# One row map instead of three, no short first loads, and loads held for gamma, in a layer-scale kernel

## The chip, the cores and the metric

The kernel runs on one core of a Trainium2 chip. The metric is device time in microseconds (us); three runs of the kernel before gave 119.6, 119.63 and 119.88 us, so its median is 119.63 us.

## The reference

`x` and `y` have the shape 1024 x 16 x 512 in bf16, `gamma` has 512 elements. All that is computed is one multiply and one add per element:

```python
def reference(x, y, gamma):
    return x + gamma * y
```

Flattened, `x`, `y` and the output are 16384 rows of 512 elements, 1 KB a row and 16.78 MB a tensor. Two tensors are read and one is written: 50.33 MB.

## The kernel before, in words

**Row map.** Each of the 128 SBUF partitions owns 128 rows, 128 KB of each tensor. Which rows is set by `BLOCKS = [4, 64, 60]` (line 7): the tensor is cut into three consecutive blocks of 128x4, 128x64 and 128x60 rows, and in a block partition p owns the p-th run of 4, 64 or 60 consecutive rows (`rows_of`, line 65). Two neighbouring partitions therefore read 4 KB, 64 KB or 60 KB apart in HBM, and a load of a whole block is one unbroken region of HBM.

**Buffers.** `y_sb` holds all 128 rows of a partition. A product is written over `y` and a sum over the product, so `y_sb` is also what is stored. `x_sb` holds 76 rows; the last number of an `x` load says where it goes. The loads of rows 68 to 120 and 120 to 128 overwrite rows of earlier loads and wait for the adds that read them (`frees`, line 102, and the wait on `s_add`, line 126).

**Queues.** `SP` (line 12) lists the loads that SyncE issues, `ACT` (line 20) the DMAs that ScalarE issues: the first four rows of `x`, `gamma` as one row of 1 KB, and three stores. The order is written out by hand, and `ring` (line 113) walks each list. All three stores wait for `s_go`, which TensorE gives once the load named in `RELEASE`, `x` rows 68 to 120, has landed (lines 157 and 158).

**Start.** `EARLY = (2, 1)` moves the first two SP loads and the first ACT load to the very beginning of the program, ahead of the barriers. `HOLD, AHEAD = ('y', 0, 4), (2, 1)` hold everything behind them, `gamma` included, until the four-row load of `y` has landed: TensorE waits for that load (line 147) and then raises one semaphore for each of SP, ACT and VectorE.

**Gamma.** A matmul of a column of ones with the row `gamma_row` spreads it over 128 partitions in PSUM (line 152), and VectorE copies it to `gamma_sb` (line 154).

**Compute.** VectorE does all elementwise work in pieces of 8, 16, 44, 52 and 8 rows (`PIECES`, line 9), in the order written in `DVE` (line 28): the multiplies (line 180) of pieces 0, 1, 2, the adds (line 189) of pieces 2, 0, 1, the multiplies of 3 and 4, the adds of 3 and 4.

Of the kernel before, what the change touches and what calls it, by code (L numbers as in the profile page):

```python
# [3 lines left out]

BLOCKS = [4, 64, 60]

PIECES = [8, 16, 44, 52, 8]


SP = [
    ('y', 0, 4),
    ('y', 4, 68),
    ('x', 4, 68, 4),
    ('y', 68, 128),
    ('x', 68, 120, 24),
    ('x', 120, 128, 0),
]
ACT = [('x', 0, 4, 0), ('g',), ('s', 4, 68), ('s', 0, 4), ('s', 68, 128)]  # L20

EARLY = (2, 1)

HOLD, AHEAD = ('y', 0, 4), (2, 1)

RELEASE = ('x', 68, 120, 24)

DVE = [('m', 0), ('m', 1), ('m', 2), ('a', 2), ('a', 0), ('a', 1), ('m', 3), ('m', 4), ('a', 3), ('a', 4)]
MULT, ADD = mybir.AluOpType.mult, mybir.AluOpType.add
# [2 lines left out]
def _take(sem, n, eng):  # L32


    return eng.wait_ge(sem, n).then_inc(sem, -n)  # L35


def kernel(
# [9 lines left out]
    nc = tc.nc  # L48
# [8 lines left out]
    rows = N // P  # L57
    n = len(PIECES)
    assert sum(PIECES) == rows
    starts = [sum(PIECES[:c]) for c in range(n + 1)]  # L60
    dt = xf.dtype
    edges = [sum(BLOCKS[:c]) for c in range(len(BLOCKS) + 1)]
    assert edges[-1] == rows

    def rows_of(t, a, b):

        c = max(c for c in range(len(BLOCKS)) if edges[c] <= a)
        assert b <= edges[c + 1]
# [6 lines left out]
    y_sb = nc.alloc_sbuf_tensor("y_sb", [P, rows, D], dt).ap()  # L75
    x_loads = [w for w in ACT + SP if w[0] == "x"]
    y_loads = [w for w in SP + ACT if w[0] == "y"]
    stores = [w for w in SP + ACT if w[0] == "s"]
    for loads in (x_loads, y_loads, stores):
# [7 lines left out]
    s_load = {w: sem("s_" + "_".join(map(str, w[:2]))) for w in x_loads + y_loads}  # L87
    s_held = {nc.sync: sem("s_held_sp"), nc.scalar: sem("s_held_act"), nc.vector: sem("s_held_dve")}
# [4 lines left out]
    def meets(a, b, c, d):  # L93
        return a < d and c < b
# [4 lines left out]
    def x_at(row):  # L99
        return next(w[3] + row - w[1] for w in x_loads if w[1] <= row < w[2])  # L100
# [12 lines left out]
    def ring(eng, what, n_early, n_ahead):  # L113

        known, went = 0, False
        for k, w in enumerate(what):
            kind = w[0]
            if k == n_ahead:
                _take(s_held[eng], 1, eng)
            need = frees(w) if kind == "x" else pieces_of(w[1], w[2]) + list(w[3:]) if kind == "s" else []  # L120
            need = max((order[c] + 1 for c in need), default=0)
            if kind == "s" and not went:
                _take(s_go, 1, eng)
                went = True
            if need > known:
                eng.wait_ge(s_add, need)
                known = need
            if kind == "g":
                i = eng.dma_start(out=gamma_row, in_=gamma.unsqueeze(0)).then_inc(s_gamma, 16)
            elif kind == "x":  # L130
                to = x_sb[:, w[3] : w[3] + w[2] - w[1], :]
                i = eng.dma_start(out=to, in_=rows_of(xf, w[1], w[2])).then_inc(s_load[w], 16)
            elif kind == "y":
                r = slice(w[1], w[2])
                i = eng.dma_start(out=y_sb[:, r, :], in_=rows_of(yf, w[1], w[2])).then_inc(s_load[w], 16)
            else:
                r = slice(w[1], w[2])
                i = eng.dma_start(out=rows_of(of, w[1], w[2]), in_=y_sb[:, r, :]).then_inc(s_out, 16)
            if k < n_early:
                early.append(i.ins)  # L140

    ring(nc.sync, SP, EARLY[0], AHEAD[0])
    ring(nc.scalar, ACT, EARLY[1], AHEAD[1])


    nc.vector.memset(ones_row, 1.0).then_inc(s_ones, 1)  # L146
    _take(s_load[HOLD], 16, nc.tensor)
    for s_one in s_held.values():
        nc.tensor.sem_inc(s_one, 1)
    _take(s_ones, 1, nc.tensor)  # L150
    _take(s_gamma, 16, nc.tensor)
    nc.tensor.matmul(gamma_ps, ones_row, gamma_row, start=True, stop=True).then_inc(s_ps, 1)  # L152
    _take(s_ps, 1, nc.vector)
    nc.vector.tensor_copy(out=gamma_sb, in_=gamma_ps).then_inc(s_dve, 1)  # L154
    _take(s_dve, 1, nc.vector)

    _take(s_load[RELEASE], 16, nc.tensor)
    nc.tensor.sem_inc(s_go, 1)
# [4 lines left out]
    def need(loads, c):  # L163
        for w in loads:
            if w not in landed and meets(starts[c], starts[c + 1], w[1], w[2]):
                if w == RELEASE:
                    _take(s_rel, 1, nc.vector)
                elif w == HOLD:
                    _take(s_held[nc.vector], 1, nc.vector)
                else:  # L170
                    _take(s_load[w], 16, nc.vector)
                landed.add(w)

    for kind, *args in DVE:
        c = args[0]
        yt = y_sb[:, starts[c] : starts[c + 1], :]
        if kind == "m":
            need(y_loads, c)
            g = gamma_sb[:, None, :].to_broadcast([P, PIECES[c], D])
            nc.vector.tensor_tensor(out=yt, in0=yt, in1=g, op=MULT).then_inc(s_dve, 1)  # L180
            open_mults += 1
        else:
# [4 lines left out]
            at = x_at(starts[c])  # L187
            xt = x_sb[:, at : at + PIECES[c], :]
            nc.vector.tensor_tensor(out=yt, in0=xt, in1=yt, op=ADD).then_inc(s_add, 1)  # L189
# [44 lines left out]
```

## Time and profile before

| what | value |
|---|---|
| median of three runs | 119.63 us (119.6 to 119.88) |
| span of the profiled execution | 118.2 us |
| runs' median less that span (around the span) | 1.4 us |
| VectorE busy | 70.1 us, 59% of the span |
| TensorE busy | 0.6 us |
| DMA | 50.33 MB, 426 GB/s over the span |
| first multiply starts | 23.95 us |
| first add starts | 43.45 us |
| first store issued | 77.41 us |
| matmul of gamma starts | 11.59 us |

The span runs from the first to the last instruction of the program. The page gives no separate whole time for the profiled execution, so 1.4 us is the distance from its span to the median of the runs. In the views below, DVE is VectorE, SPq and ACTq are the instruction streams of SyncE and ScalarE that issue DMAs, and q1 and q10 are the DMA queues that they feed. Sixteen DMA engines serve both queues. A DMA is cut into packets; the trace has start, duration, queue and size of each, and a load over 128 partitions is 128 packets, one for each partition, eight on each engine.

### The profile page before, as it was taken

The numbers are of one execution on the slowest core, as the hardware profiler recorded it, in microseconds if no ns is written. First come the engines' busy times: TensorE is split into PE (matmuls) and PEld (weight loads), VectorE is DVE, ScalarE is ACT, GpSimd is POOL, SyncE is SP. The second block draws the span as 40 slices with busy tenths as digits, with TensorE's granted clock in tenths as the row PEclk, the third lists the DMA queues.
The fourth block names the chain that finished last, engine by engine and source line by source line (L and its number), as shares of the span: only waits on it lengthen the run. The fifth ranks groups of instructions, "written<-read, shape, count | busy, mean of one in ns | idle before, by whom it ended". The sixth has DMA issues, their size and how long they took to land. (4 is left out here: it accounts for less than half of the span.)

```text
span 118.2 us, 91 instructions
## 1 busy us (share of the span) xinstructions
PE 0.6 (0%) x1; PEld 0.1 (0%) x1; DVE 70.1 (59%) x12; POOL 0.2 (0%) x4
## 2 busy tenths in 40 slices
PE   0000100000000000000000000000000000000000
PEld 0000000000000000000000000000000000000000
DVE  0000200089999969999999999999999900000000
POOL 0000000000000000000000000000000000000000
DMA  6999889988899879879969696898899889799793
GB/s 248 461 666 399 355 355 399 665 355 355 355 599 466 355 333 624 374 333 499 499 288 576 288 576 288 360 637 355 355 576 488 355 355 510 333 582 416 333 499 166
DMA packets 1442, 50.33 MB, mean 426 GB/s; under 512 B 161, under 2 KB 162, under 8 KB 546
## 3 DMA queue, kind: packets, MB, share of 16 engines
q1 hardware_dynamic: 864, 33.03, 64.8%
q10 hardware_dynamic: 578, 17.30, 33.9%
HBM read 33.56 MB, written 16.78 MB: 426 GB/s over the span
## 5 line engine op out<-in xcount | busy, mean ns | idle before, releaser
L180 DVE TENSOR_TENSOR y_sb<-y_sb,gamma_sb 128x4096 bf16<-128x4096 bf16 (+3 forms) x5 | 34.7, 6981 | 10.9 <-DVEq L35 10.9
L189 DVE TENSOR_TENSOR y_sb<-x_sb,y_sb 128x4096 bf16<-128x4096 bf16 (+3 forms) x5 | 34.7, 6981 | 1.2 <-DVEq L35 1.1
L154 DVE CAST gamma_sb<-gamma_ps 128x512 bf16<-128x512 f32 x1 | 0.7, 692 | 10.2 <-DVEq L35 10.2
L146 DVE MEMSET ones_row<- 1x128 bf16 x1 | 0.2, 165 | 2.0 <-PEq L51 2.0
L152 PE MATMUL gamma_ps<-gamma_row,ones_row 1*128 1x512 bf16 x1 | 0.6, 581 | 11.6 <-PEq L35 11.6
L152 PEld LDWEIGHTS gamma_ps<-gamma_row,ones_row 1*128 1x128 bf16 x1 | 0.1, 101 | 11.6 <-issue 11.6
L218 POOL MEMSET const-bfloat16-1.0<- 128x1 bf16 x1 | 0.1, 101 | 0.0
L218 POOL MEMSET const-uint8-127<- 128x1 uint8 x1 | 0.1, 101 | 0.0
L218 POOL MEMSET const-float32-0.0<- 128x1 f32 x1 | 0.1, 98 | 0.2 <-issue 0.2
L218 POOL MEMSET const-float32-1.0<- 128x1 f32 x1 | 0.1, 98 | 0.0
## 6 DMA issues: line engine op xcount, KB each, us to landing
y_sb<-in_y_dram SPq DMA_DIRECT2D x1, 7680.0 KB, 57.3
out_dram<-y_sb ACTq DMA_DIRECT2D x1, 7680.0 KB, 23.8
x_sb<-in_x_dram SPq DMA_DIRECT2D x1, 6656.0 KB, 21.7
x_sb<-in_x_dram SPq DMA_DIRECT2D x1, 1024.0 KB, 22.0
y_sb<-in_y_dram SPq DMA_DIRECT2D x1, 512.0 KB, 3.4
x_sb<-in_x_dram ACTq DMA_DIRECT2D x1, 512.0 KB, 4.2
out_dram<-y_sb ACTq DMA_DIRECT2D x1, 512.0 KB, 22.3
y_sb<-in_y_dram SPq DMA_DIRECT2D x1, 23.4
```

Source lines behind the costliest of these rows:

```text
L146: nc.vector.memset(ones_row, 1.0).then_inc(s_ones, 1)
L152: nc.tensor.matmul(gamma_ps, ones_row, gamma_row, start=True, stop=True).then_inc(s_ps, 1)
L154: nc.vector.tensor_copy(out=gamma_sb, in_=gamma_ps).then_inc(s_dve, 1)
L180: nc.vector.tensor_tensor(out=yt, in0=yt, in1=g, op=MULT).then_inc(s_dve, 1)
L189: nc.vector.tensor_tensor(out=yt, in0=xt, in1=yt, op=ADD).then_inc(s_add, 1)
L218: nc = _bacc.Bacc("TRN2", target_bir_lowering=False, num_devices=1)
```

## The change

- One block: partition p owns rows 128p to 128p + 127, so neighbouring partitions are 128 KB apart in every load and store.
- The four-row loads of `y` and `x` and the four-row store are gone. SP issues `y` 0 to 64, `x` 0 to 64, `y` 64 to 128, `x` 64 to 120, `x` 120 to 128; ACT issues `gamma` and two stores of 64 rows. `x_sb` still has 76 rows.
- The pieces are 8, 12, 44, 56 and 8 rows; VectorE's order is the same.
- Only the first load of `y` is issued early. All later SP loads are held until `gamma` has landed. `gamma` is held by nothing, but is not issued early either.
- `RELEASE` is now the load of `x` rows 64 to 120.

```diff
-BLOCKS = [4, 64, 60]
-PIECES = [8, 16, 44, 52, 8]
+BLOCKS = [128]
+PIECES = [8, 12, 44, 56, 8]
 SP = [
-    ('y', 0, 4),
-    ('y', 4, 68),
-    ('x', 4, 68, 4),
-    ('y', 68, 128),
-    ('x', 68, 120, 24),
+    ('y', 0, 64),
+    ('x', 0, 64, 0),
+    ('y', 64, 128),
+    ('x', 64, 120, 20),
     ('x', 120, 128, 0),
 ]
-ACT = [('x', 0, 4, 0), ('g',), ('s', 4, 68), ('s', 0, 4), ('s', 68, 128)]
-EARLY = (2, 1)
-HOLD, AHEAD = ('y', 0, 4), (2, 1)
-RELEASE = ('x', 68, 120, 24)
+ACT = [('g',), ('s', 0, 64), ('s', 64, 128)]
+EARLY = (1, 0)
+HOLD = ('g',)
+AHEAD = (1, None)
+RELEASE = ('x', 64, 120, 20)
...
     nc.vector.memset(ones_row, 1.0).then_inc(s_ones, 1)
-    _take(s_load[HOLD], 16, nc.tensor)
-    for s_one in s_held.values():
-        nc.tensor.sem_inc(s_one, 1)
     _take(s_ones, 1, nc.tensor)
     _take(s_gamma, 16, nc.tensor)
+    nc.tensor.sem_inc(s_held[nc.sync], 1)
     nc.tensor.matmul(gamma_ps, ones_row, gamma_row, start=True, stop=True).then_inc(s_ps, 1)
```

## The prediction

> **What bounds the kernel now.** I read the page first: VectorE is busy for 59% of the span, TensorE for nothing worth counting, and the DMA row has no empty slice.
>
> ```profile
> DMA  6999889988899879879969696898899889799793
> ...
> q1 hardware_dynamic: 864, 33.03, 64.8%
> q10 hardware_dynamic: 578, 17.30, 33.9%
> HBM read 33.56 MB, written 16.78 MB: 426 GB/s over the span
> ```
>
> The two queues' packets fill 64.8 + 33.9 = 98.7% of sixteen engines' span. The chain of waits names only VectorE's last adds, because it follows instructions and not packets; here it misleads. So next the busy times by stretch, cut where the loads and stores change over:
>
> ```profile
> core 0: us, PE busy (x) PEld busy (x) DVE busy (x) POOL busy (x), PEclk, DMA share, GB/s
> 0.00:1.00 1.00, 0.00 (x0) 0.00 (x0) 0.00 (x0) 0.20 (x4) 1.00 0.00 0
> 1.00:3.70 2.70, 0.00 (x0) 0.00 (x0) 0.17 (x1) 0.00 (x0) 1.00 1.15 457
> 3.70:23.00 19.30, 0.58 (x1) 0.10 (x1) 0.69 (x1) 0.00 (x0) 1.00 0.99 425
> 23.00:42.40 19.40, 0.00 (x0) 0.00 (x0) 18.43 (x3) 0.00 (x0) 1.00 1.01 436
> 42.40:60.50 18.10, 0.00 (x0) 0.00 (x0) 17.05 (x3) 0.00 (x0) 1.00 1.00 431
> ...
> 99.30:117.40 18.10, 0.00 (x0) 0.00 (x0) 0.00 (x0) 0.00 (x0) 1.00 1.00 433
> ```
>
> The last two columns count: the DMA share is 1 in every stretch from 1.00 us on (a packet counts where it starts, hence values a little over 1). The rate is the same at the 64 KB pitch of neighbouring partitions (3.7 to 42.4) and at 60 KB (42.4 to 60.5). In the packet records no engine idles for 0.2 us between its first packet (1.00 to 1.37 us, mean 1.17) and its last (ends 117.41 to 117.84, mean 117.57). The end comes when 3.15 MB have gone through each engine. A change can gain only by cheaper packets and a cheaper start, and lose by letting the engines run dry or by slower packets. The timeline tells what could run dry:
>
> ```profile
> 0.00 0.85 SPq L135 DMA_DIRECT2D y_sb<-in_y_dram  x2
> 0.13 0.38 ACTq L132 DMA_DIRECT2D x_sb<-in_x_dram  x1
> 1.99 0.17 DVE L146 MEMSET ones_row<- 1x128 bf16 x1 [1.99 <-PEq L51]
> 3.71 0.33 SPq L132 DMA_DIRECT2D x_sb<-in_x_dram  x1
> 3.90 0.50 ACTq L129 DMA_DIRECT2D gamma_row<-in_gamma_dram  x1
> 11.59 0.58 PE L152 MATMUL gamma_ps<-gamma_row,ones_row 1*128 1x512 bf16 x1 [11.59 <-PEq L35]
> 23.95 18.43 DVE L180 TENSOR_TENSOR y_sb<-y_sb,gamma_sb 128x4096 bf16<-128x4096 bf16 x3 [10.94 <-DVEq L35]
> 43.45 18.43 DVE L189 TENSOR_TENSOR y_sb<-x_sb,y_sb 128x22528 bf16<-128x22528 bf16 x3 [1.08 <-DVEq L35]
> 55.37 2.53 SPq L132 DMA_DIRECT2D x_sb<-in_x_dram  x2
> 77.41 17.36 ACTq L138 DMA_DIRECT2D out_dram<-y_sb  x3
> ```
>
> Gamma is issued at 3.90 and its matmul starts at 11.59. The 1 KB packet ran at 8.62, between the second and third 64 KB packets of its engine, and its semaphore came at 11.45, one such packet later.
>
> **Packets.** Start-to-start spacings on a busy engine: 155 ns for 4 KB, 306 for 8 KB, 1964 for 52 KB, 2264 for 60 KB, 2415 for 64 KB. Every 128-partition DMA puts eight on each engine. Before: 24 x 155 + 24 x 2415 + 16 x 2264 + 8 x 1964 + 8 x 306 = 116.06 us. After, 56 KB taken halfway between 52 and 60, at 2114: 40 x 2415 + 8 x 2114 + 8 x 306 = 115.96 us. Removing 4 KB packets is worth 0.10 us, no more; the bytes are the same. The final store keeps its place.
>
> **Start.** An engine is active for 117.57 - 1.17 = 116.40 us, 0.34 over the steady sum. Of that 0.11 lies in the two four-row loads (their first packets average 206, 180 and 182 ns against 159), 0.13 in the first five rounds of 64 KB packets (means 2481 to 2425 against 2418). A cold start with 64 KB packets is not in this trace. Bounds: all 0.24 goes (-0.24), or the first rounds are longer by what the short packets spent plus the 0.10 saved (+0.10). I take -0.06, half the head's share, because the nearest row, the first 4 KB packet, is only 47 ns over its steady value. First issue to first packet stays at 1.00: the early first SP load stays first.
>
> **The hold.** SyncE now waits for gamma instead of y 0:4, and queued behind that wait are its other four loads; whoever waits for those is VectorE's first add. Gamma itself no longer waits for anything but the barriers, so ACT issues it about when VectorE's memset runs, 2.0 us. Its engine's packets of y 0:64 begin near 1.1, 3.6, 6.0 and 8.4. With one or two of them ahead of it, gamma runs at 3.6 or 6.0 and its semaphore comes one packet and 0.36 us later, at 6.3 or 8.8 (before: packet end 11.09, semaphore 11.45). I take 8.8, the delay of before; with three packets ahead it would be 11.2. SP issues x 0:64 0.33 us after that (y 0:4 landed at 3.38, SP's next issue was 3.71), and its packets are ready 1.0 us after the issue (0.00 to 1.00). y 0:64 occupies the engines until 1.17 + 8 x 2.42 = 20.5. So x 0:64 must be issued by 19.5 and is issued at 9.1. The cost is zero, hidden by the first y load; the cover is gone once gamma lands after 19.2, and from there every us of delay is a us of the end. The gamma copy on VectorE, 1.5 us after landing, also ends well before y 0:64 lands.
>
> **VectorE and the stores.** Landings trail the last packet by 0.45 us (23.50 to 23.95). After: y 0:64 at 21.2. Multiplies of 8, 12 and 44 rows: 2.29 + 3.36 (midway between 8 and 16 rows, 2.29 and 4.42) + 11.89 = 17.5, ending at 38.7; x 0:64 lands at 40.4, so a new wait of 1.7 us appears, on an engine with room. Adds of 44, 8, 12: 52.3, 54.6, 57.9. The first of these frees x 64:120, issued at 52.3 while the engines are full until 59.1: 6.8 us of cover (now 60.5 - 55.4 = 5.1). x 120:128, freed at 54.6, stands behind it in the queue. y 64:128 lands at 59.7; 56 rows cost 14.02 x 56/52 = 15.10 and 8 rows 2.29, to 77.1; x 64:120 lands near 76.7. The adds then end at 94.5. Store 64:128 is needed at 97.7 and is ready 1.0 us after issue: 2.2 us left where 3.9 are now. Store 0:64 has the tightest place: released by x 64:120, covered by the eight 8 KB packets (2.45 us) as now, when the engines passed from load to store with no gap. Cost zero in each; if the release came later, every microsecond beyond the cover would add one.
>
> **Pitch.** All loads and stores now step 128 KB from partition to partition. The trace has 64 KB against 60 KB: 2418 ns for 65536 bytes and 2267 for 61440, both 27.1 bytes a ns. I exclude a gain, since an engine's rate is alike at both pitches and for loads and stores, so something other than the pitch sets it. Upper end: the slowest round of the trace, 2481 against 2418, for the whole kernel: 2.6% of 116 us, 3.0 us. I take zero, the nearest row being an exact tie.
>
> The row on pitch is that tie. The Trainium skill, page "DMA: Bandwidth & Descriptors", section "Latency and other measured facts", speaks against the change: copies of 16 KB tiles within HBM fell from 214 to 207 GB/s at a pitch of 512 KB and to 164 at 2 MB; 128 KB is below its table. Its 3.3% on 116 us would be an estimate of 3.8 us, 123.3 in all; the trace's tie makes it nothing, and no run here yet shows 128 KB.
>
> The row on gamma is its place after two 64 KB packets. The same page, section "Queues, rings and completion order", has an engine drain a whole packet of typically 9 to 17 descriptors from one queue before it turns to the other; by that gamma would follow all eight of y 0:64 and the time would be that of the first rival below.
>
> **Sum.** -0.10 - 0.06 = -0.16 us, on the span 118.2 and, with the same 1.4 us around it, on the median: 119.63 - 0.16 = 119.47. Own range 119.2 to 119.75: bounds -0.34 and 0.00 and the runs' spread of 0.28. About 0.3%, 0.36 us, is what a measurement of this kernel can tell from no change.
>
> **Rivals.** *Gamma waits for the whole first load (slower).* For it: the packets of x 0:4, on the second queue, began only at 2.21 to 2.56, when an engine's eight of y 0:4 were done or nearly. Against it: gamma passed six of eight queued 64 KB packets. Price: packet at 20.5, landing 20.9, SP's issue 21.2, packets 22.2: 1.7 us dry, 121.2. It decides from a landing at 19.2.
>
> *The 128 KB pitch slows packets (slower).* Against it the tie; for it, that 60 and 64 KB lie close together, so that a tie of the two says little of twice the pitch. It counts as slower from 0.52 us over the sum, 11 ns on each of 48 large packets; up to 122.5.
>
> *The start is cheaper than I take (faster).* All 0.24 of start overhead goes, and the last engine's lag over the mean (117.84 against 117.57) shrinks by 0.1: -0.44, 119.2. For it: slow first rounds follow directly on the mixed short packets of two queues. Against it: the excess of the fifth round (2449, at 13.4 us) is far from any short packet.
>
> *VectorE or the release becomes the bound.* 2.2 us of room speak against it; 0.5 us late would give 120.0.
>
> **Chances.** Forecast 0.54, cheaper start 0.20, pitch 0.14 (half of it below 120.7), gamma 0.08, VectorE 0.04. Faster 0.22, with 0.02 from the forecast's lower edge; same 0.52; slower 0.26. The range 119.1 to 120.7 leaves out gamma, half of pitch and a little of the cheap start.
>
> **What would show it.** Right: DMA share near 1 in every stretch, no gap in the load sequence at 20.5, first multiply near 21.2, first add near 40.5, gamma's matmul between 6.5 and 11.6, packets of 2418 ns. Wrong: x 0:64 issued after 19.5, an empty slice near 20 us or 78 us, 64 KB packets above 2430 ns, or a first packet later than 1.0 us.

## The result and the profile after

The changed kernel takes 119.95 us (119.72 to 120.47, 19 runs) against 119.67 us (119.6 to 120.08, 19 runs) for the kernel before: a ratio of 1.002, interval 1.0012 to 1.0028. It is 0.28 us slower; the forecast was 0.16 us faster. The profiled execution has a span of 118.7 us and a whole time of 119.98 us. First the page after, the same parts as of before:

```profile
DMA  9889888998899888988897897898899889988890
...
q1 hardware_dynamic: 720, 33.55, 65.9%
q10 hardware_dynamic: 290, 16.78, 32.6%
HBM read 33.56 MB, written 16.78 MB: 424 GB/s over the span
```

The packets fill 65.9 + 32.6 = 98.5% of the sixteen engines' span, against 98.7% before, and no slice but the last is empty; a packet counts where it starts, and only one starts there. A busy share does not tell a good packet from a slow one. The busy times by stretch do, through the rate in the last column (cut where the loads change over in the new kernel):

```profile
core 0: us, PE busy (x) PEld busy (x) DVE busy (x) POOL busy (x), PEclk, DMA share, GB/s
0.90:3.90 3.00, 0.00 (x0) 0.00 (x0) 0.17 (x1) 0.00 (x0) 1.00 1.04 350
3.90:20.80 16.90, 0.58 (x1) 0.10 (x1) 0.69 (x1) 0.00 (x0) 1.00 1.00 434
20.80:40.20 19.40, 0.00 (x0) 0.00 (x0) 17.36 (x3) 0.00 (x0) 1.00 1.00 432
40.20:59.50 19.30, 0.00 (x0) 0.00 (x0) 17.36 (x3) 0.00 (x0) 1.00 1.00 435
59.50:76.50 17.00, 0.00 (x0) 0.00 (x0) 15.80 (x2) 0.00 (x0) 1.00 1.00 432
76.50:78.90 2.40, 0.00 (x0) 0.00 (x0) 2.24 (x2) 0.00 (x0) 1.00 0.94 396
78.90:98.20 19.30, 0.00 (x0) 0.00 (x0) 16.54 (x2) 0.00 (x0) 1.00 1.01 440
98.20:117.50 19.30, 0.00 (x0) 0.00 (x0) 0.00 (x0) 0.00 (x0) 1.00 1.00 435
```

In the long stretches behind 3.9 us the engines move 432 to 440 GB/s; the 396 of the short one from loads to stores comes with a share of 0.94, because packets count where they start. In the first stretch the engines are just as busy and move 350. The DMA view cut to 0.9 to 3.9 us says why. For the changed kernel:

```profile
DMA packets 16, 1.05 MB, mean 350 GB/s; under 512 B 0, under 2 KB 0, under 8 KB 0
...
q1 hardware_dynamic: 16, 1.05, 104.4%
```

Sixteen packets, one for each engine, took 104.4% of sixteen times 3.0 us: 3.13 us each. A 64 KB packet took 2.418 us in the kernel before and takes 2.418 us in later rounds here, so the first round lost 0.71 us on an engine in the mean (0.11 to 1.00), before a second packet could start at 3.95 to 4.63 us. Nothing behind it has room to catch up: in the packet records no engine idles for more than 60 ns between two packets until the end. The timeline shows the delay handed on, and the hold paying nothing:

```profile
0.00 0.37 SPq L136 DMA_DIRECT2D y_sb<-in_y_dram  x1
...
1.43 0.52 ACTq L130 DMA_DIRECT2D gamma_row<-in_gamma_dram  x1
...
9.74 0.58 PE L151 MATMUL gamma_ps<-gamma_row,ones_row 1*128 1x512 bf16 x1 [9.74 <-PEq L36]
9.79 0.33 SPq L133 DMA_DIRECT2D x_sb<-in_x_dram  x1
...
22.02 17.36 DVE L179 TENSOR_TENSOR y_sb<-y_sb,gamma_sb 128x4096 bf16<-128x4096 bf16 x3 [10.87 <-DVEq L36]
41.46 17.36 DVE L188 TENSOR_TENSOR y_sb<-x_sb,y_sb 128x22528 bf16<-128x22528 bf16 x3 [2.07 <-DVEq L36]
53.38 2.53 SPq L133 DMA_DIRECT2D x_sb<-in_x_dram  x2
...
77.86 17.95 ACTq L139 DMA_DIRECT2D out_dram<-y_sb  x2
```

The load of x is issued at 9.79; its first packet runs at 20.89, behind the last of y 0:64 on that engine. The first multiply stands at 22.02 where 21.2 was forecast, the first add at 41.46 for 40.5: 0.8 and 1.0 us late. VectorE waits for the engine that comes last, and the slowest first packet lost 1.00 us.

### The profile page after: what moved, and what is told of

Same layout as the page of the kernel before. It is cut to its first block, busy times and chain, and to the rows that moved or that the text cites. A ratio compares the mean times of both kernels' runs of the same rounds, so it can differ in the third digit from the quotient of the medians.

```text
span 118.7 us, 82 instructions
## 1 busy us (share of the span) xinstructions
PE 0.6 (0%) x1; PEld 0.1 (0%) x1; DVE 70.2 (59%) x12; POOL 0.2 (0%) x4
## 3 DMA queue, kind: packets, MB, share of 16 engines
q1 hardware_dynamic: 720, 33.55, 65.9%
q10 hardware_dynamic: 290, 16.78, 32.6%
```

## The experiments

Each set of up to four kernels ran on one chip beside the kernel before, whose median was 119.72 or 119.73 us in every set; the sets ran on different chips. A "head" is a short first load. "Excess" is, for packets that start before 3.5 us, the time over the usual duration of their size, summed over the packet records and divided by sixteen engines. The kernel before had 0.11 us in its first trace. A ratio is the time over that of the kernel before, with its 95% interval.

**A control.** The changed kernel once more.

> The changed kernel once more, as the control for the others. In its first trace the first round of sixteen 64 KB packets took 3132 ns in the mean, against 2418 in later rounds: 0.71 us of excess. Theory A (the cold start itself: large packets into idle engines cost a fixed 0.5 to 0.7 us) and theory B (the 128 KB pitch: engines that start together read addresses 512 KB apart and collide until they have drifted apart) both expect 0.6 to 0.8 us again and a time 0.2 to 0.4 us over the kernel before. If the excess is a chance of one execution, it is under 0.3 us here.

1.0027 (1.0018 to 1.0036). First round 2967 ns, excess 0.55 us, a little under the 0.6 that was expected at least. The loss stays.

**The same without the 128 KB pitch.**

```diff
-BLOCKS = [128]
+BLOCKS = [64, 64]
```

> The changed kernel with two blocks of 64 rows, so that neighbouring partitions are 64 KB apart instead of 128 KB; nothing else moves. Theory A (cold start of large packets): first round 3050 to 3200 ns, time as the changed kernel, 0.2 to 0.4 us over the kernel before. Theory B (pitch): the collisions lessen, first round under 2800 ns, time within 0.1 us of the kernel before or up to 0.2 us faster.

1.0023 (1.0014 to 1.0032), and in the DMA view from 0.9 to 3.9 us:

```profile
q1 hardware_dynamic: 16, 1.05, 103.7%
```

3.11 us for a packet. Halving the pitch changes neither the time nor the first round. Theory B has failed here.

**The changed kernel with a head of 4 rows of y.**

```diff
-    ('y', 0, 64),
+    ('y', 0, 4),
+    ('y', 4, 64),
...
-EARLY = (1, 0)
+EARLY = (2, 0)
...
-AHEAD = (1, None)
+AHEAD = (2, None)
```

> The changed kernel with its first load split into rows 0 to 4 and 4 to 64 of y, both issued early; one row map of 128 KB pitch, no x head, loads held for gamma as in the change. Theory A (cold start of large packets): the 4 KB packets take the start, 4 KB packets average under 175 ns, the first round of large packets has less than 0.15 us of excess, the time falls 0.4 to 0.5 us under the changed kernel, 0.1 to 0.2 us under the kernel before. Theory B (pitch): the 4 KB packets, 512 KB apart between engines, collide in turn, together 0.5 us or more of excess in the first two rounds sizes, time as the changed kernel.

1.0004 (0.9994 to 1.0014): the loss was gone in this set. But the 4 KB packets averaged 202 ns, where theory A allowed 175, and their excess was 0.34 us. The repeat below takes the good time back.

**The kernel before with the new row map alone.**

```diff
-BLOCKS = [4, 64, 60]
+BLOCKS = [128]
```

> The kernel before with one block of 128 rows: the 128 KB pitch alone, with head, lists, pieces and hold of before. Theory A (cold start): within 0.1 us of the kernel before, 4 KB packets of the head under 175 ns in the mean. Theory B (pitch): the head's packets or the first 64 KB round carry 0.5 us of excess, time 0.3 to 0.5 us over the kernel before.

1.0023 (1.0014 to 1.0032), with 0.42 us of excess. The row map, with head, lists and hold of before, costs as much as the whole change. In this trace the packets that started between 30 and 60 us lost another 0.21 us (0.05 and 0.08 in the two traces of the kernel before). Theory A fails here as theory B failed without a head; the size of the first packets cannot be all of it.

**An odd pitch without a head.** The halves are cut at row 63, and the later loads, the stores and two pieces follow.

```diff
-BLOCKS = [128]
+BLOCKS = [63, 65]
...
-    ('y', 0, 64),
-    ('x', 0, 64, 0),
+    ('y', 0, 63),
+    ('x', 0, 63, 0),
...
```

> The changed kernel with its halves cut at row 63 instead of 64, in two blocks of 63 and 65 rows: the first load is 63 KB from each partition at a pitch of 63 KB, no power of two. Theory B (engines that start together collide because their addresses lie a power of two apart): first round of the large packets under 2650 ns (its steady value is near 2380). Theory C (what costs is the reach of the first packets: sixteen places far apart, touched for the first time with nothing queued to hide it, whatever the exact distance) and theory A (the size of the first packets): 2900 to 3150 ns, as at 64 and 128 KB.

3055 ns against 2380 steady, an excess of 0.68 us, in one execution. A pitch that is a power of two is not needed for a slow first round.

**The head of before, 68 KB apart.**

```diff
-BLOCKS = [4, 64, 60]
+BLOCKS = [68, 60]
```

> The kernel before with blocks of 68 and 60 rows instead of 4, 64 and 60: its four-row head keeps its 4 KB packets, but they lie 68 KB apart instead of 4 KB, and not a power of two. With the head at 128 KB its first round took 406 ns and the head's excess was 0.45 us; at 4 KB 205 ns and 0.11 us. Theory B (powers of two): first round under 260 ns, excess under 0.2 us, time as the kernel before. Theory C (reach): first round 350 to 450 ns, excess 0.3 to 0.5 us, time 0.2 to 0.3 us over the kernel before. Theory A (size of the first packets alone): as the kernel before.

The trace went with theory C, the time did not: first round 353 ns and 0.36 us of excess, yet 1.0002 (0.9993 to 1.0011), the time that theories A and B expected.

**Heads of 16 rows**, first near together, then 128 KB apart. The first edits the kernel before; the head of x, its store and the hold grow to 16 rows with it:

```diff
-BLOCKS = [4, 64, 60]
+BLOCKS = [16, 52, 60]
...
-    ('y', 0, 4),
-    ('y', 4, 68),
-    ('x', 4, 68, 4),
+    ('y', 0, 16),
+    ('y', 16, 68),
+    ('x', 16, 68, 16),
...
```

> The kernel before with a head of 16 rows instead of 4, in a block of its own: 16 KB packets at a pitch of 16 KB, blocks of 16, 52 and 60 rows; all else as before. Theory C (reach): the first sixteen packets span 1.9 MB instead of 0.5, excess of the head somewhat over the 0.11 us of before, 0.15 to 0.35 us. Theory A (size): excess scales with the size between 0.11 us at 4 KB and 0.7 us at 64 KB, 0.2 to 0.35 us. Time within 0.2 us of the kernel before.

The second edits the changed kernel:

```diff
-    ('y', 0, 64),
+    ('y', 0, 16),
+    ('y', 16, 64),
...
-EARLY = (1, 0)
+EARLY = (2, 0)
...
-AHEAD = (1, None)
+AHEAD = (2, None)
```

> The changed kernel with its first load split into rows 0 to 16 and 16 to 64, both issued early: 16 KB packets at the 128 KB pitch. Theory C (reach): excess of the 16 KB packets 0.35 to 0.6 us, clearly over that of the same packets at a pitch of 16 KB. Theory A (size): the same excess as 16 KB packets at a pitch of 16 KB, to 0.1 us.

Near: 1.0015 (1.0007 to 1.0024), excess 0.42 us, over the 0.35 that both theories allowed. Far: 0.51 us in one trace. The distance is worth about 0.1 us of excess at this size, as theory A has it. Theory S in the next expectation is theory A drawn more finely: large packets that come first into idle engines cost about 0.6 us, and small packets ahead of them spare most of it. Timed, the second gave:

> The changed kernel with a head of 16 rows of y (16 KB packets at the 128 KB pitch), now timed. Its first trace had 0.54 us of excess in these packets, against 0.37 us with 4 KB packets at the same pitch and 0.69 to 0.78 us without a head. Theory S: the time lies between the two, 0.1 to 0.25 us over the kernel before. Rival (any split of the first load repairs the loss): within 0.07 us of the kernel before.

1.0004 (0.9995 to 1.0013), with 0.54 us of excess. Theory S, which put it 0.1 to 0.25 us over the kernel before, missed, and the far head, with more excess, was faster than the near one. The rival that any split repairs the loss was within its bound here; the heads of 2, 8 and again 4 rows below came out beyond it.

**The large load first, the 4-row load behind it.** The same number of loads queued early as with the 4-row head.

```diff
-    ('y', 0, 64),
+    ('y', 0, 60),
+    ('y', 60, 64),
...
-EARLY = (1, 0)
+EARLY = (2, 0)
...
-AHEAD = (1, None)
+AHEAD = (2, None)
```

> The changed kernel with its first load split into rows 0 to 60 and 60 to 64 of y, both issued early: as many early loads as in the version with a head of 4 rows, but the large one first. Theory S (large packets that come first into idle engines cost about 0.6 us, and a load of 4 KB packets ahead of them spares most of it): first round of 60 KB packets 2750 to 3000 ns against 2267 steady, time 0.2 to 0.35 us over the kernel before. Rival Q (it helps that two loads are queued early, whichever comes first): first round under 2450 ns, time within 0.1 us of the kernel before.

1.0031 (1.0021 to 1.0040). The DMA view from 0.9 to 3.9 us:

```profile
q1 hardware_dynamic: 16, 0.98, 101.4%
```

3.04 us for a 60 KB packet that takes 2.267 later, a little over theory S's range. A second load in the queue does not help; what comes first into the idle engines carries the loss.

**No hold.**

```diff
-AHEAD = (1, None)
+AHEAD = (None, None)
...
-    nc.tensor.sem_inc(s_held[nc.sync], 1)
```

> The changed kernel without its hold: SyncE issues x 0 to 64 and y 64 to 128 as soon as it is past the barriers, and only gamma's matmul waits for gamma. Theory S: the hold is hidden by the first load and costs nothing, so the time stays 0.2 to 0.3 us over the kernel before, first round again near 3100 ns, gamma lands 6 to 12 us after the start. Rival (the hold, or gamma's place among the loads, makes part of the loss): at least 0.15 us faster than the changed kernel.

1.0025 (1.0016 to 1.0034), the same loss. The timeline:

```profile
1.42 0.33 SPq L133 DMA_DIRECT2D x_sb<-in_x_dram  x1
1.43 0.53 ACTq L130 DMA_DIRECT2D gamma_row<-in_gamma_dram  x1
...
1.80 0.50 SPq L136 DMA_DIRECT2D y_sb<-in_y_dram  x1
...
9.68 0.58 PE L150 MATMUL gamma_ps<-gamma_row,ones_row 1*128 1x512 bf16 x1 [9.68 <-PEq L36]
```

Two loads are now queued from 1.4 and 1.8 us on, and gamma's matmul starts at 9.68 instead of 9.74. The hold neither costs nor buys anything that the runs can tell. In the profiled execution, at 120.33 us the slowest of its twelve, packets that started between 30 and 90 us lost another 0.47 us (0.04 in the changed kernel): a loss can also arise behind the start.

**The kernel before, a second trace.**

> The kernel before once more, for a second trace of its start. In its first trace the head's 4 KB packets had 0.11 us of excess and the large packets behind it 0.15 us. Theory S: head 0.05 to 0.2 us again, under the 0.37 to 0.45 us of the same packets 68 or 128 KB apart. If the reach of the head's packets makes no difference and the first trace was a lucky one: 0.3 us or more.

119.67 us, excess 0.26 us, between the two expectations. The sixteen packets that start first, in the first trace (0.90 to 1.255 us) and in this one (0.90 to 1.32):

```profile
q1 hardware_dynamic: 16, 0.07, 58.0%
```

```profile
q1 hardware_dynamic: 16, 0.07, 86.7%
```

0.580 x 0.355 = 0.206 us and 0.867 x 0.42 = 0.364 us a packet, with the same code. The 0.11 of the first trace was at the low end; even so the start of this head, 4 KB apart, lost less than every other that was tried, the nearest by 0.09 us (0.35, one trace).

**The row map once more, and its wide pitch without its wide head.** The second edit is:

```diff
-BLOCKS = [4, 64, 60]
+BLOCKS = [4, 124]
```

> The kernel before with the single row map, again: the first time it took 1.0023 of the kernel before, though a 4-row head at the same pitch in the changed kernel's lists took 1.0004 and the kernel before with blocks of 68 and 60 rows 1.0002. Theory S (only the size of the first packets matters) expects 1.000 to 1.001 and calls the first result chance. Rival P (the 128 KB pitch costs in its own right when both queues start with a head) expects 1.002 to 1.003 again.

> The kernel before with blocks of 4 and 124 rows: the head as it was, 4 KB apart, and everything behind it at a pitch of 124 KB. Theory S: within 0.1% of the kernel before. Rival P in the form that the wide pitch of the large loads costs: 1.0015 or more, with large loads' packets 5 ns or more over those of the kernel before in the mean; in the form that only 128 KB does, as theory S.

1.0022 (1.0013 to 1.0030) and 1.0027 (1.0015 to 1.0040). The first confirms that the row map costs by itself in the lists of before. The second is not settled: its time is that of rival P, but its 64 KB packets averaged 2421 ns against 2422 before, so not the 5 ns more that went with it. Its profiled execution took 119.7 us, the shortest of twelve, with 0.28 us of excess, while its runs spread to 120.42.

**Smaller heads in the changed kernel**, split at row 2 and, in the same way, at row 8.

```diff
-    ('y', 0, 64),
+    ('y', 0, 2),
+    ('y', 2, 64),
...
-EARLY = (1, 0)
+EARLY = (2, 0)
...
-AHEAD = (1, None)
+AHEAD = (2, None)
```

> The changed kernel with a head of 2 rows of y, 2 KB packets. Theory S by size of the first packet: at most as much startup loss as with 4 rows, 0.1 to 0.35 us of excess in the head; the large packets behind it then start sooner, 0.35 us after the first, and may carry some of the loss themselves (first large round up to 0.3 us over steady). Time 0.999 to 1.001 of the kernel before. If the loss is tied to the time since the first packet and not to its size, the first large round carries 0.3 us or more and the time is 1.0015 or more.

> The changed kernel with a head of 8 rows of y, 8 KB packets at the 128 KB pitch. Theory S: between 4 and 16 rows, 0.35 to 0.55 us of excess in the head, next to none in the large packets behind it, time 0.9995 to 1.001 of the kernel before.

1.0017 for both (1.0004 to 1.0030, 1.0003 to 1.0031). With 2 KB packets the head's excess was 0.24 us, and the first round of 62 KB packets behind it took 2.73 us in the mean, up to 3.1, against 2.342: another 0.38 us. Both signs of the alternative, that the loss is tied to the time since the first packet, came in (0.3 us or more, 1.0015 or more), though the interval of the time reaches down to 1.0004. A head that is over after about 1 us hands part of the loss on to the large packets. With 8 KB packets the excess was 0.52 us.

**The head of 4 rows again, and at 64 KB.** The first is the kernel with that head as above; the second adds to it:

```diff
-BLOCKS = [128]
+BLOCKS = [64, 64]
```

> The changed kernel with a head of 4 rows of y, a second time: the first gave 1.0004 of the kernel before, 8 rows 1.0017, 16 rows 1.0004, all at the 128 KB pitch. Theory S (the first packets' size): 0.9995 to 1.0010, as the first time. Rival P (the wide pitch costs 0.2% by itself, and the first result was chance): 1.0015 to 1.0025.

> The same kernel with two blocks of 64 rows, so that head and large loads step 64 KB; no 4-row load of x and no 4-row store, unlike the kernel before. Without its head this kernel took 1.0023. Theory S: 0.999 to 1.0008. Theory S with rival P (wide pitch costs as well): here under the run at 128 KB by 0.1% or more. If neither head nor pitch explains the loss but the lists do: 1.0015 or more.

1.0025 (1.0016 to 1.0034) and 1.0065 (1.0052 to 1.0079). The first contradicts its earlier 1.0004 with the same code on another chip, and theory S with it. The same 4-row load, cut to the stretch in which the sixteen first packets start, in the first set (0.90 to 1.41 us), in this one (0.90 to 1.53) and at 64 KB (0.90 to 1.40):

```profile
q1 hardware_dynamic: 16, 0.07, 76.9%
```

```profile
q1 hardware_dynamic: 16, 0.07, 94.3%
```

```profile
q1 hardware_dynamic: 16, 0.07, 145.2%
```

0.769 x 0.51 = 0.39 us, 0.943 x 0.63 = 0.59 us and 1.452 x 0.50 = 0.73 us for a 4 KB packet that takes 0.159 us when the engines run. The excess of the whole start was 0.35, 0.52 and 0.74 us. The last of these is the slowest kernel of the study, in five runs. Its start lost no more than that of the changed kernel (0.71), so the start does not explain 1.0065; its trace has another 0.24 us of excess after 3.5 us (0.07 in the changed kernel), and the rest is open. No version beat the kernel before.

## Why the prediction was wrong, by its steps

**Packets: right.** 64 KB packets took 2418 ns at the 128 KB pitch and 56 KB packets 2116, as the steady sum had them, so its saving of 0.10 us stands.

**The hold: right.** Gamma ran at 6.63 us, behind two 64 KB packets of its engine, and landed at 9.42, where 8.8 was forecast plus the late start. x 0:64 was issued 10 us before it was needed, and without the hold nothing changed. The rival that gamma waits for the whole first load fell. Here the arbitration rule of the Trainium skill, page "DMA: Bandwidth & Descriptors", section "Queues, rings and completion order" (an engine drains some 9 to 17 descriptors of one queue before it switches), does not describe what two queues with 64 KB packets did: gamma passed six of eight, before and after.

**VectorE and the stores: right.** The waits grew as told (1.7 us before the first add was forecast, 2.07 measured), and no store came late.

**Pitch: right for the steady packets, wrong as a whole.** The usual packet behind the start did not get slower. But the rival was priced as slow packets throughout; the row map alone, in the kernel before, cost 0.22 to 0.23%, with 0.42 and 0.43 us of excess in the start against 0.11 and 0.26. A price of the pitch that falls on the first packets was in none of the cases.

**Start: the step that failed.** It was taken at -0.06 us, with bounds of -0.24 and +0.10, although the prediction says that no cold start with 64 KB packets is in its trace. The nearest row that I chose was the first 4 KB packets, 47 ns over their steady value, and I carried those nanoseconds over to a packet sixteen times as large. The row was also that of one execution: in the second trace of the same kernel these packets were 205 ns over. The first 64 KB packets were 714 ns over, and 549 in the control. Summed over all loads and both traces of each kernel, the excess went from 0.31 and 0.46 us to 0.78 and 0.62: +0.32 in the mean. The engines' first packets started at 1.17 (the prediction's figure) and 1.13 us and now start at 1.17 and 1.26: +0.07. With the 0.10 saved that is +0.29 us, against +0.24 between the mean ends of the engines in these four traces and +0.28 between the medians. So the start cost about 0.4 us where a gain of 0.06 was put. The upper bound was short because the trace of before held no large packet on idle engines, and the bound was made from small ones instead of from what a first large packet can lose at most.

**What is shown and what is open.** Shown: in the changed kernel the loss is made by the first round of packets (0.71 of 0.78 us, in the control 0.55 of 0.62) and is still there at the end. It comes at pitches of 63, 64 and 128 KB alike, with the hold and without it, and the usual duration of later packets has no part in it. Starts on partitions whose rows lie 63 KB or more apart, or with packets of 8 KB or more, lost 0.35 to 0.77 us in every trace; the head of before, 4 KB packets 4 KB apart, lost 0.11 to 0.28.

Open is the mechanism. Open is also the part of the pitch in the kernels with a head: timed, 68 KB (1.0002) was better than 128 KB (1.0022 and 1.0023), and 4 KB with 124 KB behind it (1.0027) was not. The changed kernel's lists with a head that lies near together were not tried. The same 4-row head gave 1.0004 on one chip and 1.0025 on another.

The excess at the start does not order the times by itself. At the 64 KB pitch without a head, 0.69 us were lost and that execution took 119.79 us; with the 4-row head 0.35 us were lost and it took 119.84, because its last engine ended 0.37 us after the mean engine instead of 0.20. And one trace is one execution: those with 0.36 and 0.54 us of excess (68 KB apart; 16 rows) took 119.86 and 119.89 us, above the medians of 119.75 and 119.80 that seemed to contradict them. Excess and time of a kernel vary between executions by as much as the effect.

## What to carry to other kernels

Where the DMA engines never pause, what the first packets lose is not made up later: read the rate of the first stretch, not its busy share. Do not price a cold first packet from a small one's excess, least of all from one trace. In nanoseconds the 4 KB row gave 47 where 64 KB packets lost 714; as a share, 30%, it would have come close, but only by luck, since the second trace of the same packets had 129%. A short load that lies close together in HBM lost least at the start, but with wide rows behind it the kernel took 1.0027, so it is a thing to try and not a rule. A difference of 0.2% needs sets on more than one chip before a repair is believed.

## What the runs showed of the hardware

- First 64 KB packets on sixteen idle engines took 2.53 to 3.42 us in the changed kernel's first trace, against 2.418 later, and the shortest of them was that of an engine which started only at 1.92 us; the others lost at least 0.52 us. In the control the two that started at 1.77 and 1.90 us took 2.42 and 2.45 us.
- First 16 KB packets behaved alike: 1.0 to 1.1 us in the mean against 0.611, while in the near head two that started at 1.61 and 1.99 us took 0.608 and a third at 2.03 took 1.04. A late start does not spare the loss in every case: behind a head of 2 KB packets, 62 KB packets that started between 1.74 and 2.53 us took 2.73 us in the mean against 2.342.
- In steady state pitches of 60, 63, 64, 68, 124 and 128 KB made no difference to the median packet: 27.1 bytes a ns on each engine, for loads and stores.
